# Attention, then two feed-forward layers on one core: the queries of two batches in one tile, and the epsilon and reciprocal of several head pairs in one instruction each

## The chip, the cores and the metric

The kernel runs on one NeuronCore of a Trainium2 chip. TensorE (PE in the views; PEld is its weight load), VectorE (DVE), ScalarE (ACT) and GpSimd (POOL) compute, SyncE (SP) issues the DMAs. The metric is device microseconds of one execution; before the change the median of three runs is 859.54 us (859.41 to 859.98).

## The reference, cut to what matters

```
q_s = exp(q - max(q, axis=-1)); q_s /= sum(q_s, axis=-1) + 1e-9     # over the 64 of a head
k_s = exp(k - max(k, axis=2));  k_s /= sum(k_s, axis=2) + 1e-9      # over the sequence
kv  = einsum('bhsd,bhse->bhde', k_s, v)                             # 64 x 64 per head
out = einsum('bhsd,bhde->bhse', q_s, kv)                            # 4 batches, 8 heads, 576 x 64
x   = out as 2304 tokens x 512
h = x @ w_in1;  x = (h * sigmoid(h)) @ w_out1                       # 512 -> 2048 -> 512
h = x @ w_in2;  y = (h * tanh(softplus(h))) @ w_out2
```

## The kernel before

**Tiling.** Eight heads are worked as four pairs (`hp` 0 to 3), so that 2 x 64 fills 128 partitions. The 2304 tokens are cut into six blocks of 384. A batch has 576 tokens, so block 1 holds 192 tokens of batch 0 and 192 of batch 1, block 4 those of batches 2 and 3; the other four lie within one batch. Weights and activations are split into a high and a low part, so that each product is three TensorE passes. In the first half of layer 1 a block needs eight groups of hidden units: for each group a first product "G1" (12 matmuls of 128x384, `psum<-xs,wall`), ScalarE's SiLU (`gf<-psum`), VectorE's high part (`CAST g`) and low part (`TENSOR_TENSOR g`), and a second product "G2" (12 matmuls, `psum<-g,wall`). I call them matmuls of the layer, and number the groups c0 to c7.

**Order.** `events` writes out G1 and G2 with G2 three groups behind G1 (`SKEW`), and each has a time in steps (`at`). Attention of the next blocks is a generator (`attn_steps`) whose pieces get times from `PACE`; a scheduler fixes the order on each engine from these times when the program is built, and then every engine works in order. The first block's attention is written out by hand in `START`. While block 0 is computed, the 16 weight pieces of the half are loaded (four buffers `st`, issued by SP in order), put together from two integer halves and split (`TENSOR_SCALAR st`, `ACTIVATE wt`, `SCALAR_TENSOR_TENSOR wt`, `CAST wall`, `TENSOR_TENSOR wall`): five instructions for each piece. Attention of block 1 runs in the same stretch, and block 1's G1 can't begin before it is done.

**Attention of a block.** `load` issues K, Q and V of a head pair. `front` (two head pairs at a time, four for block 2) turns K on TensorE, takes its maximum on VectorE (`knm`), the exponential with its sum on ScalarE (`kT_exp`, `kz`), and for the queries the maximum (`qmx`, VectorE), the subtraction (GpSimd) and the exponential (ScalarE). `back` takes a head pair: it turns the exponential of K back (`ke_turn`, `ke_copy`), forms `kv` on TensorE (`kv_prod`) and scales it (`kvf`, VectorE), sums the queries (`qz`, `qrz`, VectorE), divides (`qn`, GpSimd), turns (`qT`) and multiplies them with `kvf`. SiLU and the exponential are of different ScalarE tables, so going from one to the other puts an `ACT_TABLE_LOAD` into ScalarE's order.

Two buffers bind the order: G1 writes two PSUM banks in turn, `banks("h1", (4, 5))`, so G1 of group c waits for `gf` of group c-2; and `gf` has two buffers, so `gf` of c waits for the low part of c-2. Where a block has queries of two batches, each batch's queries are a tile of 96x256 of their own, and each is summed by

```
V.tensor_reduce(out=z, in_=qt, op=ALU.add, axis=AX.X)
V.tensor_scalar(out=z, in0=z, scalar1=EPS, scalar2=None, op0=ALU.add)
V.reciprocal(out=rz, in_=z)
```

Of the kernel before, what the change touches and what calls it, by code (L numbers as in the profile page):

```python
# [7 lines left out]
F32 = mybir.dt.float32  # L8
# [3 lines left out]
ALU = mybir.AluOpType  # L12
# [3 lines left out]
EPS = 1e-9  # L16
# [49 lines left out]
def attention_silu_mish(ctx: ExitStack, tc: tile.TileContext, q, k, v, w_in1, w_out1, w_in2, w_out2, out):  # L66
# [28 lines left out]
    TURN = 2  # L95


    X_LEAD, W_LEAD, T_LAG, P_LAG, A_END = 7, 8.0, 3.0, 4.0, 8.0
    X_NEAR = SKEW + 2


    W_EVERY, W_WAIT = 4.0, 8
    PACE = (0.5, 1.05)

    START = """
        A0 A1 M0 M1 Q0 B0 K0 B1 A2 C0 M2 A3 P2 M3 Q1 K1
        S0 E0 P4 R0 P3 C1 B2 Q2 K2 P2 Z0 B3 Q3 S1 N0 E1
        Z2 D1 S2 Z3 R1 C2 S3 Z1 N1 T0 E2 D0 K3 T1 R2 E3
        F0 U0 N2 X0 R3 C3 D2 U1 N3 F1 H0 T2 Y0 L0 T3 D3
        F2 F3 U2 U3 P2 X1 H1 Y1 X3 L1 H3 Y3 X2 H2 L3 L2  # L110
        Y2
    """.split()

    const = ctx.enter_context(tc.tile_pool(name="const", bufs=1))
# [243 lines left out]
    def room(parts, n):  # L358
        at = first["at"]
        first["at"] += n  # L360
        return xb[:parts, at:at + n]
# [34 lines left out]
            SP.dma_start(va[:, h, :, 0:D], v[b, 2 * hp + h].rearrange("(p r) d -> p r d", r=KR))  # L396
        return va

    def load_q(j, b, hp, s0, pn, rn):
        n = 2 * rn * D  # L400
        if j == 0:
            qt = room(pn, n)
        elif j == 1:
            qt = later(xb, hp, NT - (1 + (s0 == 0)) * n, pn, n)
        elif j == 2:
            qt = later(xa, hp, 3 * BLK, pn, n)
        else:
            qt = qp_.tile([pn, n], F32, tag="qt", name="qt")
        qt = qt.rearrange("p (h r d) -> p h r d", h=2, d=D)
        SP.dma_start(  # L410
            qt.rearrange("p h r d -> p h (r d)"),
            q[b, 2 * hp:2 * hp + 2, s0:s0 + pn * rn].rearrange("h (p r) d -> p h (r d)", r=rn),
        )
        return qt


# [11 lines left out]
        V.tensor_reduce(out=nm, in_=kT, op=ALU.max, axis=AX.XY, negate=True)  # L428
        return nm

    def kT_exp(kT, nm, hp):
        ek = spare_ek(hp)
        z = sp_.tile([P, 1], F32, tag="kz", name="kz")
        last = S.activation(
            out=ek.rearrange("p (i n) -> p i n", i=2), in_=kT, func=ACTF.Exp, bias=nm, accum_out=z
        )
        return ek, z, last

    def kT_sum(z):
        V.tensor_scalar(out=z, in0=z, scalar1=EPS, scalar2=None, op0=ALU.add)  # L440
        rz = sp_.tile([P, 1], F32, tag="krz", name="krz")
        V.reciprocal(out=rz, in_=z)
        return rz

# [56 lines left out]
        t = qt.rearrange("p h r d -> p (h r d)")  # L501
        S.activation(out=t, in_=t, func=ACTF.Exp)

    def q_sum(qt):
        z = sp_.tile(list(qt.shape[:3]), F32, tag="qz", name="qz")
        V.tensor_reduce(out=z, in_=qt, op=ALU.add, axis=AX.X)
        V.tensor_scalar(out=z, in0=z, scalar1=EPS, scalar2=None, op0=ALU.add)
        rz = sp_.tile(list(qt.shape[:3]), F32, tag="qrz", name="qrz")
        V.reciprocal(out=rz, in_=z)
        return rz  # L510

    def q_norm(qt, rz, qn=None):
        pn, _, rn, _ = qt.shape
# [37 lines left out]
    def attn_start():  # L551

        n = BLK
        rn = n // P
        kt, qt, va = {}, {}, {}
        for hp in range(NP):
            kt[hp] = load_k(0, hp)
        for hp in range(NP):
            qt[hp] = load_q(0, 0, hp, 0, P, rn)
# [3 lines left out]
        qn = [room(P, 2 * rn * D) for _ in range(NP)]  # L563
        st = {}

        def step(what, hp):
            def do(f, *args):
                st[what, hp] = f(*args)

            def got(what):  # L570
                return st[what, hp]

            if what == "A":
                do(kT_turn, kt[hp])
            elif what == "M":
                do(kT_max, got("A"))
            elif what == "B":
                do(kT_exp, got("A"), got("M"), hp)
            elif what == "Z":
                do(kT_sum, got("B")[1])  # L580
            elif what == "K":
                do(ke_turn, got("B")[0])
            elif what == "C":
                do(ke_copy, got("K"), kt[hp])
            elif what == "D":
                do(kv_prod, kt[hp], va[hp])
            elif what == "F":
                kvs[(0, hp)] = kv_scale(got("D"), got("Z"))
            elif what == "Q":
                do(q_max, qt[hp])  # L590
            elif what == "S":
                do(q_sub, qt[hp], got("Q"))
            elif what == "E":
                do(q_exp, qt[hp])
            elif what == "R":
                do(q_sum, qt[hp])
# [26 lines left out]
        InOrder.on = False  # L623
# [4 lines left out]
    def attn_steps(j, new, parts):  # L628

        turn = new is not None and new < TURN  # L630
        ld, mid = {}, {}

        def load(hp):
            kt = load_k(new, hp) if new is not None else None
            qs = [load_q(j, b, hp, s0, *shape(n)) for b, s0, n in parts]
            va = load_v(new, hp) if new is not None else None
            ld[hp] = (kt, va, qs)

        def front(hps):
            last = None  # L640
            for hp in hps:
                kt, va, qs = ld[hp]
                if turn:
                    kT = kT_turn(kt)
                    ek, z, last = kT_exp(kT, kT_max(kT), hp)
                    mid[hp] = ek, kT_sum(z)
                elif kt is not None:
                    k_max(kt)
                for qt in qs:
                    q_sub(qt, q_max(qt))  # L650
                yield
            for hp in hps:
                kt, va, qs = ld[hp]
                if kt is not None and not turn:
                    last = k_exp(kt)
            with tc.issue_after(last.ins) if last is not None else ExitStack():
                for hp in hps:
                    for qt in ld[hp][2]:
                        q_exp(qt)

        def back(hp):
            kt, va, qs = ld[hp]
            rz = None
# [4 lines left out]
            qn = q_norm(qs[0], q_sum(qs[0]))
            if kt is not None:
                kvs[(new, hp)] = kv_scale(kv_prod(kt, va), rz)  # L670
                yield
            for i, (b, s0, n) in enumerate(parts):
                cur = qn
                if i + 1 < len(parts):
                    qn = q_norm(qs[i + 1], q_sum(qs[i + 1]))
                base = tc.cur_priority
                tc.cur_priority = base + int(1000 * T_LAG)
                t = q_copy(q_turn(cur))
                tc.cur_priority = base + int(1000 * P_LAG)
                px = x_prod(t, kvs[(b, hp)])  # L680
                rn, t0 = cur.shape[1], b * SEQ + s0
                S.copy(tokens(xaT[:, hp, t0:t0 + n], rn), queries(px, rn))
                tc.cur_priority = base
                yield

        wide = NP if j == 2 else 2
        for hp in range(wide):
            load(hp)
        for h0 in range(0, NP, wide):
            yield from front(range(h0, h0 + wide))  # L690
            yield
            for hp in range(h0, h0 + wide):
# [407 lines left out]
```

## Time and profile before

| | |
|---|---|
| median of three runs | 859.54 us (859.41 to 859.98) |
| the profiled execution | 862.39 us, of which 859.1 us is the span from the first to the last instruction |
| TensorE busy | 842.5 us, 98% of the span, granted clock 1.00 |
| VectorE busy | 467.4 us, 54% |
| ScalarE busy | 364.6 us, 42% |
| GpSimd busy | 54.3 us, 6% |

A row of a timeline begins with the start (us from the span's start) and the duration; `x12` merges twelve like instructions; the bracket tells how long the engine was idle just before and which instruction ended that. The shapes of matmuls are those of the two operands; some merged rows count a transposition twice, as weight and as data.

### The profile page before, as it was taken

How to read it: one execution, taken by the hardware profiler on the slowest of the kernel's cores; microseconds unless marked ns; L12 is line 12 of the kernel's file. 1: busy time of each engine (PE TensorE's matmuls, PEld its weight loads, DVE VectorE, ACT ScalarE, POOL GpSimd, SP SyncE). 2: the span in 40 equal slices, each digit the busy share in tenths (PEclk: the TensorE clock that was granted, in tenths of full speed). 3: DMA queues.
4: the chain of work that ended last, by engine and by line, in shares of the span. 5: the costliest groups of instructions: out<-in, count | busy, mean ns of one | idle time of the engine just before them, and what ended most of it. 6: DMA issues, size and time to landing. Idle time of an engine off the chain costs nothing.

```text
span 859.1 us, 12311 instructions
## 1 busy us (share of the span) xinstructions
PE 842.5 (98%) x4666; PEld 755.1 (88%) x4666; DVE 467.4 (54%) x1004; ACT 364.6 (42%) x702; POOL 54.3 (6%) x82
## 2 busy tenths in 40 slices
PE   7899999999999999999999999999999999999998
PEld 6688989899999887898888899998999998999996
DVE  4998556673257556556474656675343454343431
ACT  5987354555244644435434444444322233322221
POOL 3144211221000000000000000000000000000000
PEclk9999999999999999999999999999999999999999
DMA  9995411120023428675632778889555455664312
GB/s 227 249 261 109 100 32 44 47 65 1 1 74 124 147 88 288 204 252 165 218 128 88 273 275 302 296 323 340 216 172 232 152 204 184 232 219 161 135 50 98
DMA packets 86105, 145.49 MB, mean 169 GB/s; under 512 B 33056, under 2 KB 60192, under 8 KB 82976
## 3 DMA queue, kind: packets, MB, share of 16 engines
q1 hardware_dynamic: 86048, 144.73, 51.9%
q8 instruction: 36, 0.59, 0.3%
q14 instruction: 21, 0.17, 0.1%
HBM read 105.38 MB, written 39.32 MB: 168 GB/s over the span
## 4 chain that ended last, share of the span: by engine, by line
PE 87%; DVE 5%; DMA 3%; ACT 2%; SPq 1%; issue 1%; ACTq 0%; DVEq 0%
PE psum L59 70%; PE psum L57 17%; DMA st<-in_moe_w_in_dram 2%; SPq L57 1%; DMA st<-in_moe_w_out_dram 1%; DVE g L57 1%; DVE qz L57 1%; DVE kmx L57 1%; DVE wall L57 0%; ACT xa L57 0%; DVE wt L59 0%; DVE st L57 0%; DVE xs L59 0%; DVE wt L57 0%; DVE xs L57 0%
## 5 line engine op out<-in xcount | busy, mean ns | idle before, releaser
L59 PE MATMUL psum<-wall,g 128*128 128x512 f32 x864 | 210.1, 390 | 0.0
L59 PE MATMUL psum<-x,wall 128*128 128x384 f32 x1008 | 191.8, 338 | 0.0
L59 PEld LDWEIGHTS psum<-wall,g 128*128 128x128 f32 x864 | 161.3, 188 | 28.5 <-DVE xb L59 0.3
L59 PEld LDWEIGHTS psum<-x,wall 128*128 128x128 f32 x1008 | 179.9, 187 | 6.8
L59 PE MATMUL psum<-g,wall 128*128 128x512 f32 (+2 forms) x624 | 129.0, 360 | 0.0
L59 PE MATMUL psum<-xs,wall 128*128 128x512 f32 (+2 forms) x588 | 122.7, 362 | 0.5 <-ACT gf L59 0.5
L59 PEld LDWEIGHTS psum<-g,wall 128*128 128x128 f32 x624 | 109.0, 188 | 14.7
L59 PEld LDWEIGHTS psum<-xs,wall 128*128 128x128 f32 x588 | 102.7, 188 | 15.8 <-ACT gf L59 0.9
L59 DVE TENSOR_TENSOR hf<-psum,sc 128x384 f32<-128x384 f32 x72 | 40.0, 556 | 123.4 <-ACT sc L59 79.0
L57 PE MATMUL psum<-xs,wall 128*128 128x384 f32 x468 | 98.3, 350 | 2.7 <-ACT gf L57 1.9
L59 ACT COPY sc<-psum 128x384 f32<-128x384 f32 x72 | 34.5, 479 | 133.0 <-PE psum L59 133.0
L57 PEld LDWEIGHTS psum<-xs,wall 128*128 128x128 f32 x468 | 80.3, 189 | 6.8 <-ACT gf L57 2.8
L57 PE MATMUL psum<-g,wall 128*128 128x384 f32 x432 | 84.8, 343 | 1.3 <-DVE g L57 1.3
L57 PEld LDWEIGHTS psum<-g,wall 128*128 128x128 f32 x432 | 74.7, 188 | 2.7 <-DVE g L57 1.8
L59 ACT ACTIVATE hf<-hf 128x384 f32<-128x384 f32 x72 | 37.8, 526 | 84.6 <-DVE hf L59 84.6
L59 DVE TENSOR_TENSOR g<-gf,g 128x512 fp32r<-128x512 f32 (+2 forms) x49 | 30.5, 623 | 74.7 <-ACT g L59 74.4
L59 ACT ACTIVATE gf<-psum 128x512 f32<-128x512 f32 (+2 forms) x49 | 26.6, 543 | 98.4 <-PE psum L59 97.4
L59 DVE CAST g<-hf 128x384 fp32r<-128x384 f32 x96 | 34.6, 360 | 58.1 <-ACT hf L59 57.7
L59 DVE TENSOR_TENSOR g<-hf,g 128x384 fp32r<-128x384 f32 x96 | 53.6, 559 | 3.3
L59 ACT ACTIVATE wt<-st 128x512 f32<-128x512 f32 x48 | 32.0, 676 | 19.5 <-DMA st<-in_moe_w_in_dram 10.7
L57 DVE CAST g<-gf 128x384 fp32r<-128x384 f32 x39 | 16.7, 427 | 38.7 <-ACT gf L57 38.6
L57 ACT ACTIVATE gf<-psum 128x384 f32<-128x384 f32 x39 | 18.9, 491 | 41.0 <-PE psum L57 39.3
(123 smaller groups left out, 747.1 us busy)
## 6 DMA issues: line engine op xcount, KB each, us to landing
wall<-wq SPq DMA_DIRECT2D x16, 1792.0 KB, 7.4
st<-in_moe_w_in_dram SPq DMA_DIRECT2D x32, 512.0 KB, 5.2
st<-in_moe_w_out_dram SPq DMA_DIRECT2D x32, 512.0 KB, 4.3
wall<-wo SPq DMA_DIRECT2D x32, 512.0 KB, 3.6
wq<-wall SPq DMA_DIRECT2D x8, 1792.0 KB, 6.2
wo<-wall SPq DMA_DIRECT2D x16, 512.0 KB, 5.6
wqf<-wt SPq DMA_DIRECT2D x24, 256.0 KB, 3.3
wall<-wqf SPq DMA_DIRECT2D x24, 256.0 KB, 6.5
```

The costliest lines, as they stand in the source:

```text
L57: return call(*args, **kwargs)
L59: self.last = call(*args, **kwargs)
```

## The change

1. `load_q` puts the queries of both batches of a block into one tile (96x512 in place of two of 96x256), still with one DMA each. Maximum, subtraction, exponential and sum of such a tile are then one instruction in place of two.
2. The epsilon and the reciprocal of the K sums are taken for two head pairs at once (`inverse`, 128x2), and those of the query sums for all head pairs that `front` takes together: 96x16 for blocks 1 and 4, 128x12 for 3 and 5, 128x24 for block 2. `q_sums` is called at the first of them, so no head pair's queries are divided before all of them have their exponential.
3. Constants of the order: `X_LEAD` 7 to 6, `PACE` (0.5, 1.05) to (0.35, 1.05), and the table `START` is written anew from its third line on.

```
-    X_LEAD, W_LEAD, T_LAG, P_LAG, A_END = 7, 8.0, 3.0, 4.0, 8.0
+    X_LEAD, W_LEAD, T_LAG, P_LAG, A_END = 6, 8.0, 3.0, 4.0, 8.0
-    PACE = (0.5, 1.05)
+    PACE = (0.35, 1.05)
...
-        Z2 D1 S2 Z3 R1 C2 S3 Z1 N1 T0 E2 D0 K3 T1 R2 E3
+        Z2 D1 S2 R1 C2 S3 N1 T0 E2 D0 F0 K3 T1 R2 E3 U0
...
-    def load_q(j, b, hp, s0, pn, rn):
+    def load_q(j, hp, parts, pn, rn):
         n = 2 * rn * D
+        m = len(parts) * n
...
+            qt = qp_.tile([pn, m], F32, tag="qt", name="qt")
+        qt = qt.rearrange("p (h r d) -> p h r d", r=rn, d=D)
+        for i, (b, s0, _) in enumerate(parts):
+            SP.dma_start(
+                qt[:, 2 * i:2 * i + 2].rearrange("p h r d -> p h (r d)"),
...
-    def kT_sum(z):
+    def inverse(z, tag):
         V.tensor_scalar(out=z, in0=z, scalar1=EPS, scalar2=None, op0=ALU.add)
-        rz = sp_.tile([P, 1], F32, tag="krz", name="krz")
+        rz = sp_.tile(list(z.shape), F32, tag=tag, name=tag)
         V.reciprocal(out=rz, in_=z)
...
-    def q_sum(qt):
-        z = sp_.tile(list(qt.shape[:3]), F32, tag="qz", name="qz")
-        V.tensor_reduce(out=z, in_=qt, op=ALU.add, axis=AX.X)
-        V.tensor_scalar(out=z, in0=z, scalar1=EPS, scalar2=None, op0=ALU.add)
...
+    def q_sums(qts):
+        h, r = qts[0].shape[1:3]
+        z = sp_.tile([qts[0].shape[0], len(qts), h * r], F32, tag="qz", name="qz")
+        for i, qt in enumerate(qts):
+            V.tensor_reduce(out=z[:, i].rearrange("p (h r) -> p h r", r=r), in_=qt, op=ALU.add, axis=AX.X)
+        rz = inverse(z, "qrz")
...
     def front(hps):
...
-                for qt in qs:
-                    q_sub(qt, q_max(qt))
+                q_sub(qt, q_max(qt))
                 yield
+            if turn:
+                rz = inverse(z, "krz")
+                for hp in hps:
+                    mid[hp] = mid[hp], rz[:, hp - hps[0]:hp - hps[0] + 1]
...
-        def back(hp):
+        def back(hp, hps):
...
-            qn = q_norm(qs[0], q_sum(qs[0]))
+            if hp == hps[0]:
+                qz.update(zip(hps, q_sums([ld[i][2] for i in hps])))
+            zq = qz.pop(hp)
+            qn = q_norm(qt[:, :2], zq[:, :2])
...
-                    qn = q_norm(qs[i + 1], q_sum(qs[i + 1]))
+                    qn = q_norm(qt[:, 2 * i + 2:2 * i + 4], zq[:, 2 * i + 2:2 * i + 4])
```

What this makes of the order, engine by engine: the orders differ from the first block's attention up to the 709th matmul of the layer (in block 3) and are the same behind it. Counted over the program, VectorE has 62 instructions fewer, GpSimd 8 and ScalarE 8 fewer, but ScalarE has 27 table loads in place of 23.

Place 1 is ScalarE in block 0. `xb,kz<-psum,knm` is the exponential of K of block 1's second head pair, `xb<-xb` that of its queries, `gf` the SiLU. Before, the first `gf` here is that of c2 and the last that of c3:

```order
L57 ACT_TABLE_LOAD
L57 ACTIVATE gf<-psum 128x384
L57 ACT_TABLE_LOAD
L57 ACTIVATE xb,kz<-psum,knm 128x576
L57 ACTIVATE xb<-xb 96x256 x3
L57 CAST wall<-wt 128x512
L57 ACTIVATE xb<-xb 96x256
L57 COPY xa<-psum 96x768
L57 ACTIVATE wt<-st 128x512 x3
L57 CAST wall<-wt 128x512
L57 ACT_TABLE_LOAD
L57 ACTIVATE gf<-psum 128x384
```

After the change the three `gf` are those of c1, c2 and c3:

```order
L57 ACT_TABLE_LOAD
L57 ACTIVATE gf<-psum 128x384
L57 ACT_TABLE_LOAD
L57 ACTIVATE xb,kz<-psum,knm 128x576
L57 ACTIVATE xb<-xb 96x512 x2
L57 CAST wall<-wt 128x512
L57 COPY xa<-psum 96x768
L57 ACTIVATE wt<-st 128x512 x2
L57 ACT_TABLE_LOAD
L57 ACTIVATE gf<-psum 128x384
L57 CAST wall<-wt 128x512 x2
L57 ACTIVATE gf<-psum 128x384
```

So the SiLU of c2 has moved from ahead of the second head pair's exponentials to behind them.

Place 2 is TensorE in the same stretch. `ident,xa` turns K, `ident,xb` turns its exponential back, `xb,xa` is `kv`. Eight matmuls of the layer stand ahead of these rows. Before:

```order
L57 MATMUL psum<-xs,wall 128x384 x19
L57 MATMUL psum<-ident,xa 128x96 x6
L57 MATMUL psum<-xs,wall 128x384 x21
L57 MATMUL psum<-g,wall 128x384 x8
L57 MATMUL psum<-ident,xa 128x96 x6
L57 MATMUL psum<-g,wall 128x384 x7
L57 MATMUL psum<-xs,wall 128x384 x12
L57 MATMUL psum<-g,wall 128x384
L57 MATMUL psum<-ident,xb 96x128 x6
L57 MATMUL psum<-g,wall 128x384 x10
L57 MATMUL psum<-xb,xa 64x64 x12
```

After the change (ahead of these rows stand 17 matmuls of the layer and the first head pair's turning of K):

```order
L57 MATMUL psum<-xs,wall 128x384 x19
L57 MATMUL psum<-g,wall 128x384 x7
L57 MATMUL psum<-ident,xa 128x96 x6
L57 MATMUL psum<-g,wall 128x384 x5
L57 MATMUL psum<-xs,wall 128x384 x12
L57 MATMUL psum<-g,wall 128x384
L57 MATMUL psum<-ident,xb 96x128 x6
L57 MATMUL psum<-g,wall 128x384 x9
L57 MATMUL psum<-xb,xa 64x64 x12
L57 MATMUL psum<-g,wall 128x384
L57 MATMUL psum<-ident,qn 128x96 x2
L57 MATMUL psum<-g,wall 128x384
```

The first G2 stood behind 48 matmuls of G1 and stands behind 36; the first `kv` of block 1 stood behind 86 matmuls of the layer and stands behind 70.

Place 3 is VectorE where the first two head pairs of block 1 are summed. Before:

```order
L57 TENSOR_SCALAR kz<-kz 128x1
L57 TENSOR_REDUCE qz<-xb 96x4
L57 RECIPROCAL krz<-kz 128x1
L57 TENSOR_REDUCE qz<-xb 96x4
L57 TENSOR_SCALAR qz<-qz 96x4
L57 TENSOR_REDUCE qz<-xb 96x4
L57 RECIPROCAL qrz<-qz 96x4
L57 TENSOR_TENSOR wall<-wt,wall 128x512
L57 TENSOR_SCALAR qz<-qz 96x4
L57 TENSOR_SCALAR st<-st 128x512
L57 RECIPROCAL qrz<-qz 96x4
L57 TENSOR_SCALAR qz<-qz 96x4
```

After the change (what stood further up or down for the same two head pairs before is in these rows now):

```order
L57 TENSOR_SCALAR kz<-kz 128x2
L57 TENSOR_SCALAR st<-st 128x512
L57 RECIPROCAL krz<-kz 128x2
L57 TENSOR_REDUCE qz<-xb 96x8 x2
L57 TENSOR_TENSOR wall<-wt,wall 128x512
L57 TENSOR_SCALAR qz<-qz 96x16
L57 TENSOR_SCALAR st<-st 128x512
L57 RECIPROCAL qrz<-qz 96x16
```

For these two head pairs four sums have become two, and six pairs of epsilon and reciprocal two.

## Rows read from the trace of the kernel before

**Rows 1.** The page: busy time of each engine, and forty slices of the span.

```profile
PE 842.5 (98%) x4666; PEld 755.1 (88%) x4666; DVE 467.4 (54%) x1004; ACT 364.6 (42%) x702; POOL 54.3 (6%) x82
...
PE   7899999999999999999999999999999999999998
```

**Rows 2.** Stages: us, busy PE, PEld, DVE, ACT, POOL, clock, DMA share, GB/s.

```profile
52.63:85.69 33.06, 31.28 (x242) 26.80 (x242) 29.57 (x73) 25.30 (x54) 15.41 (x20) 1.00 0.71 163
41.57:85.69 44.12, 41.63 (x324) 36.42 (x324) 40.56 (x103) 35.76 (x71) 19.33 (x25) 1.00 0.78 189
...
150.00:200.00 50.00, 49.70 (x362) 45.95 (x361) 33.52 (x94) 29.42 (x54) 12.42 (x19) 1.00 0.20 49
```

**Rows 3.** Timeline of TensorE, blocks 0 and 1.

```profile
39.38 0.86 PE L57 MATMUL psum<-g,wall 128*128 128x384 f32 x4
41.57 0.97 PE L57 MATMUL psum<-g,wall 128*128 128x384 f32 x4 [1.33 <-DVE g L57]
44.12 2.24 PE L57 MATMUL psum<-xs,wall 128*128 128x384 f32 x12
52.63 1.68 PE L57 MATMUL psum<-xs,wall 128*128 128x384 f32 x8 [0.72 <-ACT gf L57]
83.10 0.59 PE L57 MATMUL psum<-qT,kvf 128*128 128x192 f32 x2 [0.73 <-DVE kvf L57]
85.69 3.53 PE L57 MATMUL psum<-xs,wall 128*128 128x384 f32 x18
95.44 2.24 PE L57 MATMUL psum<-xs,wall 128*128 128x384 f32 x12
97.52 2.24 PE L57 MATMUL psum<-g,wall 128*128 128x384 f32 x12
```

**Rows 4.** Timeline of VectorE, block 0.

```profile
40.20 0.43 DVE L57 TENSOR_SCALAR st<-st 128x512 uint32<-128x512 uint32 x1 [0.36 <-DMA st<-in_moe_w_out_dram]
40.55 0.97 DVE L57 TENSOR_TENSOR g<-gf,g 128x384 fp32r<-128x384 f32 x1
43.07 0.76 DVE L57 TENSOR_REDUCE knm<-psum 128x1 f32<-128x576 f32 x1
46.38 0.42 DVE L57 TENSOR_REDUCE qz<-xb 96x4 f32<-96x256 f32 x1
46.71 0.15 DVE L57 RECIPROCAL krz<-kz 128x1 f32<-128x1 f32 x1
46.78 0.40 DVE L57 TENSOR_REDUCE qz<-xb 96x4 f32<-96x256 f32 x1
48.16 0.57 DVE L57 TENSOR_SCALAR qz<-qz 96x4 f32<-96x4 f32 x1
```

**Rows 5.** Timeline of ScalarE, block 0, and one row of block 3.

```profile
42.88 0.49 ACT L57 ACTIVATE gf<-psum 128x384 f32<-128x384 f32 x1
43.91 1.28 ACT L57 ACT_TABLE_LOAD   x1 [0.53 <-DVE knm L57]
45.20 0.74 ACT L57 ACTIVATE xb<-psum,knm 128x576 f32<-128x576 f32 x1
45.93 1.02 ACT L57 ACTIVATE xb<-xb 96x256 f32<-96x256 f32 x3
46.85 0.61 ACT L57 CAST wall<-wt 128x512 fp32r<-128x512 f32 x1
47.68 0.79 ACT L57 COPY xa<-psum 96x768 f32<-96x768 f32 x1
48.37 1.83 ACT L57 ACTIVATE wt<-st 128x512 f32<-128x512 f32 x3
50.80 1.28 ACT L57 ACT_TABLE_LOAD   x1
52.09 0.49 ACT L57 ACTIVATE gf<-psum 128x384 f32<-128x384 f32 x1
...
173.24 0.49 ACT L57 ACTIVATE gf<-psum 128x384 f32<-128x384 f32 x1 [0.70 <-PE psum L57]
```

More of the change, by code (lines that the diff above doesn't have):

```diff
@@ L107, in attention_silu_mish @@
         S0 E0 P4 R0 P3 C1 B2 Q2 K2 P2 Z0 B3 Q3 S1 N0 E1
-        Z2 D1 S2 Z3 R1 C2 S3 Z1 N1 T0 E2 D0 K3 T1 R2 E3
-        F0 U0 N2 X0 R3 C3 D2 U1 N3 F1 H0 T2 Y0 L0 T3 D3
-        F2 F3 U2 U3 P2 X1 H1 Y1 X3 L1 H3 Y3 X2 H2 L3 L2
-        Y2
+        Z2 D1 S2 R1 C2 S3 N1 T0 E2 D0 F0 K3 T1 R2 E3 U0
+        N2 X0 R3 C3 D2 U1 N3 F1 H0 T2 Y0 L0 T3 D3 F2 F3
+        U2 U3 P2 X1 H1 L1 Y1 X3 H3 Y3 X2 H2 L3 L2 Y2
     """.split()
@@ L397, in load_v @@
         return va
-    def load_q(j, b, hp, s0, pn, rn):
+    def load_q(j, hp, parts, pn, rn):
         n = 2 * rn * D
+        m = len(parts) * n
         if j == 0:
-            qt = room(pn, n)
+            qt = room(pn, m)
         elif j == 1:
-            qt = later(xb, hp, NT - (1 + (s0 == 0)) * n, pn, n)
+            qt = later(xb, hp, NT - m, pn, m)
         elif j == 2:
-            qt = later(xa, hp, 3 * BLK, pn, n)
+            qt = later(xa, hp, 3 * BLK, pn, m)
         else:
[L408 to L413, printed above, removed]
+            qt = qp_.tile([pn, m], F32, tag="qt", name="qt")
[3 more added lines that the diff above has]
+                qt[:, 2 * i:2 * i + 2].rearrange("p h r d -> p h (r d)"),
+                q[b, 2 * hp:2 * hp + 2, s0:s0 + pn * rn].rearrange("h (p r) d -> p h (r d)", r=rn),
+            )
         return qt
@@ L429, in kT_max, with kT_exp @@
         return nm
-    def kT_exp(kT, nm, hp):
+    def kT_exp(kT, nm, hp, z):
         ek = spare_ek(hp)
-        z = sp_.tile([P, 1], F32, tag="kz", name="kz")
         last = S.activation(
@@ L436, in kT_exp @@
         )
-        return ek, z, last
-    def kT_sum(z):
+        return ek, last
+    def inverse(z, tag):
         V.tensor_scalar(out=z, in0=z, scalar1=EPS, scalar2=None, op0=ALU.add)
-        rz = sp_.tile([P, 1], F32, tag="krz", name="krz")
+        rz = sp_.tile(list(z.shape), F32, tag=tag, name=tag)
         V.reciprocal(out=rz, in_=z)
@@ L502, in q_exp @@
         S.activation(out=t, in_=t, func=ACTF.Exp)
-    def q_sum(qt):
-        z = sp_.tile(list(qt.shape[:3]), F32, tag="qz", name="qz")
-        V.tensor_reduce(out=z, in_=qt, op=ALU.add, axis=AX.X)
-        V.tensor_scalar(out=z, in0=z, scalar1=EPS, scalar2=None, op0=ALU.add)
-        rz = sp_.tile(list(qt.shape[:3]), F32, tag="qrz", name="qrz")
-        V.reciprocal(out=rz, in_=z)
-        return rz
+    def q_sums(qts):
[4 more added lines that the diff above has]
+        rz = inverse(z, "qrz")
+        return [rz[:, i].rearrange("p (h r) -> p h r", r=r) for i in range(len(qts))]
     def q_norm(qt, rz, qn=None):
@@ L558, in attn_start @@
         for hp in range(NP):
-            qt[hp] = load_q(0, 0, hp, 0, P, rn)
+            qt[hp] = load_q(0, hp, [(0, 0, n)], P, rn)
         for hp in range(NP):
@@ L563, in attn_start @@
         qn = [room(P, 2 * rn * D) for _ in range(NP)]
+        kz = sp_.tile([P, NP], F32, tag="kz", name="kz")
         st = {}
@@ L577, in step @@
             elif what == "B":
-                do(kT_exp, got("A"), got("M"), hp)
+                do(kT_exp, got("A"), got("M"), hp, kz[:, hp:hp + 1])
             elif what == "Z":
-                do(kT_sum, got("B")[1])
+                rz = inverse(kz[:, hp:hp + 2], f"krz{hp}")
+                st["Z", hp], st["Z", hp + 1] = rz[:, :1], rz[:, 1:]
             elif what == "K":
@@ L595, in step @@
             elif what == "R":
-                do(q_sum, qt[hp])
+                st["R", hp], = q_sums([qt[hp]])
             elif what == "N":
@@ L630, in attn_steps @@
         turn = new is not None and new < TURN
-        ld, mid = {}, {}
+        ld, mid, qz = {}, {}, {}
         def load(hp):
             kt = load_k(new, hp) if new is not None else None
-            qs = [load_q(j, b, hp, s0, *shape(n)) for b, s0, n in parts]
+            qt = load_q(j, hp, parts, *shape(parts[0][2]))
             va = load_v(new, hp) if new is not None else None
-            ld[hp] = (kt, va, qs)
+            ld[hp] = (kt, va, qt)
         def front(hps):
@@ L641, in front @@
             for hp in hps:
-                kt, va, qs = ld[hp]
+                kt, va, qt = ld[hp]
                 if turn:
                     kT = kT_turn(kt)
-                    ek, z, last = kT_exp(kT, kT_max(kT), hp)
-                    mid[hp] = ek, kT_sum(z)
+                    if hp == hps[0]:
+                        z = sp_.tile([P, len(hps)], F32, tag="kz", name="kz")
+                    ek, last = kT_exp(kT, kT_max(kT), hp, z[:, hp - hps[0]:hp - hps[0] + 1])
+                    mid[hp] = ek
                 elif kt is not None:
                     k_max(kt)
-                for qt in qs:
-                    q_sub(qt, q_max(qt))
+                q_sub(qt, q_max(qt))
                 yield
+            if turn:
+                rz = inverse(z, "krz")
+                for hp in hps:
+                    mid[hp] = mid[hp], rz[:, hp - hps[0]:hp - hps[0] + 1]
             for hp in hps:
-                kt, va, qs = ld[hp]
+                kt, va, qt = ld[hp]
                 if kt is not None and not turn:
@@ L657, in front @@
                 for hp in hps:
-                    for qt in ld[hp][2]:
-                        q_exp(qt)
-        def back(hp):
-            kt, va, qs = ld[hp]
+                    q_exp(ld[hp][2])
+        def back(hp, hps):
+            kt, va, qt = ld[hp]
             rz = None
@@ L667, in back @@
                 yield
[L668 removed]
+            if hp == hps[0]:
+                qz.update(zip(hps, q_sums([ld[i][2] for i in hps])))
+            zq = qz.pop(hp)
+            qn = q_norm(qt[:, :2], zq[:, :2])
             if kt is not None:
@@ L692, in attn_steps @@
             for hp in range(h0, h0 + wide):
-                yield from back(hp)
+                yield from back(hp, range(h0, h0 + wide))
                 if hp + wide < NP:
```

## The prediction

> **What bounds the kernel now.** I read the page first. TensorE is busy for 98% of the span, and its first slice apart its busy digits are 8 and 9 all the way [rows 1]. 859.1 - 842.5 leaves 16.6 us of idle time, and only in it can this change find anything, because it takes no matmul away. So the next view is busy time by stage [rows 2]: between 150 and 200 us, where blocks 2 and 3 run with attention beside them, TensorE idles for 0.3 us of 50. From 41.57 to 85.69 it idles for 44.12 - 41.63 = 2.5 us while VectorE is busy for 40.56 of 44.12 and ScalarE for 35.76. That is block 0, with 16 weight pieces to put together and block 1's attention to finish. The change has to pay there or nowhere.
>
> The timeline of TensorE shows what the idle time waits for [rows 3]: 1.33 us ahead of 41.57 for the first group's low part, which stands on VectorE behind a weight piece that landed at 40.20 [rows 4]; 0.72 us ahead of 52.63 for a SiLU; 0.73 us ahead of 83.10 for a `kvf`. From 85.69 on the matmuls of the layer follow at full pace, twelve in 97.52 - 95.44 = 2.08 us, 0.1733 us each.
>
> I take 85.69 as the marker. By the order, 198 matmuls of the layer and all of block 1's attention are then done, and some of block 2's: five transpositions and one product, which take about 1.2 us up to 85.69. Without those the stretch would have ended at 84.5. From there TensorE is the bound in both kernels and does the same work, so what the marker shifts, the end shifts.
>
> **What the change removes.** In block 1's attention VectorE loses 16 of the small instructions (4 for K, 12 for the queries). One takes 0.07 to 0.09 us from start to start (46.71 to 46.78) [rows 4]; by 0.08 that is 1.3 us. Eight pairs of 96x256 reductions become eight of 96x512. One takes 46.71 - 46.38 = 0.33 us; 96x512 is not in the trace, so it lies between 0.33 and 0.66, and I take 0.60, since the length in elements is most of the price at this size: 8 x 0.06 = 0.5 us. Block 2's attention loses six more small ones, 0.5 us. Sum 2.3 us of VectorE up to the marker. The four saved in `START` are worth nothing: VectorE waits for the first weight piece right behind them. Blocks 3 to 5 lose as much again, where VectorE is busy for 33.52 of 50 us [rows 2]: nothing, as the matmuls cover it.
>
> At 48.16 one small instruction takes 0.57 us, where one at 46.71 takes 0.15 [rows 4], while GpSimd works. Half as many GpSimd instructions, each up to twice as long, can make that better or worse by up to half a us; I count 0.
>
> Where rule and row must be weighed: the Trainium skill, Perfetto Trace Analysis, "Optimizing Scalar/DVE Operations", says that larger operations help a saturated engine, and that breaking operations up can help where VectorE or ScalarE isn't saturated but makes others wait. The first half would put the gain at the whole 2.3 us; the second speaks against merging, and no row here decides between them.
>
> **What the new order adds.** This is the term that eats the gain. Up to the first group's low part nothing gets much earlier: it still stands behind the ninth weight piece. On TensorE 48 + 4 matmuls of the layer stood ahead of that wait, and now 36 + 4 do. Behind it, the SiLU of c2 was the next thing of ScalarE at 42.88 [rows 5], and G1 of c4 began at 44.12 [rows 3]. Now that SiLU stands behind the second head pair's exponentials. Its chain, by rows:
> - 41.57 to 43.07, rest of G2 and the turning of K up to `knm`: 1.5 us; one matmul fewer now, so 1.3 [rows 3, 4]
> - `knm` 0.76 [rows 4], table load 1.28, exponential of K 0.74 [rows 5]
> - two exponentials of 96x512: three of 96x256 take 0.92 us from start to start, so 0.31 each; twice that is the upper bound and 0.31 the lower; I take 0.55 each, 1.1
> - cast 0.51, copy 0.69, two weight activations at 0.6 each 1.2, table load 1.28, SiLU 0.49 [rows 5]
>
> Sum 9.35 us. From the low part at 41.5 that is 50.8. The ninth piece's DMA is issued when the fifth piece has been put together, which now has one piece's work less ahead of it, so the low part may come up to 0.7 us earlier: G1 of c4 begins between 50.1 and 50.8, and I take 50.5.
>
> By the order 72 matmuls of the layer are done at that moment. Before, 96 were at 52.63. So 126 are left to the marker, and not 102. The rest is taken from the stage 52.63 to 85.69 [rows 2]: busy 31.28, less 102 x 0.1733 = 17.7, less block 2's 1.2, is 12.4 us of attention, which does not change. The marker then lies at 50.5 + 126 x 0.1733 + 12.4 = 84.7 plus whatever TensorE waits behind 50.5. Before, it waited 33.06 - 31.28 = 1.8 us in that stage. It should wait less: VectorE has 2.3 us less to do in a stage in which it had 3.5 us to spare, and the last `kvf` now stands behind 179 matmuls of the layer in place of 197. But some of the waits are ScalarE's. Between 0 and 1.8 I take 0.6. Marker 85.3, against 84.5: 0.8 us later. The attention is ahead, the matmuls of the layer are behind, and the saving on VectorE fills the difference nearly.
>
> **Block 3.** Four more table loads, 4 x 1.28 = 5.1 us of ScalarE, all in the stage in which it is busy for 29.42 of 50 us. The SiLU of c0 in block 3, at 173.24 before [rows 5], now has an exponential of block 5's queries and two loads ahead of it. Its bank is needed by G1 of c2, some 2.5 us behind it (an estimate: the twelve matmuls of c1 at 0.1733 and two or three of attention). I count 0 and give the case a chance below. The Trainium skill, ScalarE: Activation LUTs, "What ACT_TABLE_LOAD costs", gives about 2.66 us for each switch, a drain included; the row of 43.91 shows the exponential begin 1.29 us later, so the rows bear out 1.28, and by the page the four would come to 10.6 us.
>
> **Sum.** The profiled execution was 862.39 us, span 859.1, so 3.3 us lie around the span, and it stands 2.85 us above the median. Its span would become 859.1 + 0.8 = 859.9. Set on the median of 859.54 that is 860.3 us. What a measurement of this kernel can tell from no change is about 0.2%, 1.7 us; I forecast no change that can be told.
>
> **The rivals.**
> - VectorE decides: it is busy for 92% of the stretch, and if its order, not TensorE's, sets when block 1 may begin, the 2.3 us come off whole, and TensorE makes up the matmuls in waits that go. For it: the 1.33 and 0.73 us are both waits for VectorE. Against it: TensorE needs 84.7 us by the sum above without any wait. It needs G1 of c4 by 49 us. 859.54 - 2.3 = 857.2 us. Chance 0.24.
> - The late SiLU decides: G1 of c4 begins at 51.4 or later (a ninth piece that lands late, since the K loads now stand ahead of two weight pieces in SP's order), and TensorE waits as long behind it as before, 1.8 us. Marker 51.4 + 21.8 + 12.4 + 1.8 = 87.4, 2.9 us late: 862.4 us. It decides from G1 of c4 at 51.4 with 0.8 us of waits. For it: the ScalarE chain has no slack. Chance 0.22.
> - The table loads of block 3 decide: if block 5's queries arrive 2 us after ScalarE's turn comes, the SiLUs of c0 and c1, G1 of c2 and c3 wait in turn. A load, an exponential and a load, 1.28 + 0.55 + 1.28 = 3.1 us, less 2.5 of slack, and the 2 us of lateness: about 2.6 us on top of 0.8, 862.9 us. Against it: these loads depend on tiles that come free early. Chance 0.07.
>
> **How the numbers follow.** The forecast, 860.3 us, has 0.47; its own range is 858.6 to 861.3. The range reaches to both sides, from 856.8 (2.3 us and half a us fewer collisions on VectorE off 859.54) to 863.0, just past the last rival. Faster by over 0.2% (under 857.8) is the first rival, 0.24; slower by over 0.2% (above 861.3) the other two, 0.29; the rest is within 0.2%, 0.47.
>
> **What would show it.** In the profile after: G1 of c4 (the first matmuls `psum<-xs,wall` behind the first `qn` transpositions) at about 50.5, with an idle time ahead of it that waits for a SiLU; an idle time of some 3 us on TensorE ahead of the first G2, near 38 to 41 us; VectorE's busy time about 4 us lower over the span; the first G1 of block 1 about 82 to 83 us, with 48 matmuls in one run; no idle time over 0.3 us in block 3. I am wrong if G1 of c4 begins before 49.5 or the span is below 857.3, and on the other side if TensorE waits for more than 1.5 us between 50 and 86 us.

## The result: slower, and the profile after

The changed kernel takes 866.71 us (median of six executions, 863.53 to 867.50), the kernel before beside it 859.59 us; the ratio is 1.0067, 95% interval 1.0056 to 1.0078. That is slower, above the range given. (The two medians alone lie further apart, by 7.1 us or 0.83%; the table below uses the ratio.) The profiled execution took 864.52 us with a span of 862.7, 3.6 us more than before. All six executions have a mean granted clock of 0.994 to 0.996; the profiled one before had 0.999.

The page of the changed kernel, busy time of each engine and the first slices of the span (compare [rows 1]):

```profile
PE 844.1 (98%) x4666; PEld 758.0 (88%) x4666; DVE 464.6 (54%) x942; ACT 369.7 (43%) x698; POOL 50.1 (6%) x74
...
PE   8799999999999999999999999999999999999998
```

VectorE is busy for 2.8 us less and TensorE for 1.6 us more, though it has the same matmuls. So some of them ran slower. Busy time by stage, with the granted clock in the third column from the right, tells which (the first three rows are from a table by single us):

```profile
38.00:39.00 1.00, 0.00 (x0) 0.00 (x0) 0.92 (x2) 0.95 (x3) 0.00 (x0) 1.00 1.29 195
40.00:41.00 1.00, 0.30 (x1) 0.30 (x2) 0.97 (x3) 0.98 (x2) 0.10 (x1) 0.50 1.17 208
46.00:47.00 1.00, 1.00 (x6) 1.00 (x6) 1.00 (x1) 0.99 (x2) 0.83 (x1) 0.84 1.24 197
...
40.70:46.30 5.60, 5.60 (x20) 5.50 (x21) 3.70 (x7) 2.58 (x3) 0.51 (x1) 0.50 1.15 250
52.92:88.39 35.47, 32.84 (x253) 29.30 (x254) 29.94 (x55) 25.64 (x53) 8.88 (x14) 1.00 0.71 177
150.00:200.00 50.00, 49.79 (x377) 45.94 (x378) 29.05 (x70) 31.93 (x52) 10.67 (x16) 1.00 0.20 46
```

From about 39.5 to 46.3 us the granted clock is 0.50, the lower of TensorE's two levels, 1.2 GHz in place of 2.4. Block 3, where the four added table loads lie, is undisturbed: 0.21 us idle in 50. TensorE's timeline of the changed kernel, against [rows 3]:

```profile
34.49 2.37 PE L57 MATMUL psum<-xs,wall 128*128 128x384 f32 x12 [1.11 <-ACT gf L57]
40.70 2.61 PE L57 MATMUL psum<-g,wall 128*128 128x384 f32 x7 [3.85 <-DVE g L57]
43.11 1.16 PE L57 MATMUL psum<-ident,xa 96*128 96x96 f32 x6
43.98 1.95 PE L57 MATMUL psum<-g,wall 128*128 128x384 f32 x5
52.92 2.01 PE L57 MATMUL psum<-xs,wall 128*128 128x384 f32 x10 [0.66 <-ACT gf L57]
85.21 0.59 PE L57 MATMUL psum<-qT,kvf 128*128 128x192 f32 x2 [1.87 <-DVE kvf L57]
88.39 8.48 PE L57 MATMUL psum<-xs,wall 128*128 128x384 f32 x48
```

The 3.85 us ahead of the first G2 are the idle time that was expected there. Behind it seven G2 matmuls take 43.11 - 40.70 = 2.41 us, 0.344 each; at the full clock one takes 0.1733 [rows 3]. The turning of the second head pair's K is late by that, VectorE's `knm` with it, and with `knm` ScalarE's chain up to the SiLU of c2. G1 of c4 begins at 52.92. A second large wait, 1.87 us, stands at the end of block 0 ahead of the last products of block 1's attention. VectorE ahead of the first G2 before the change (one row), and then at both places in the changed kernel:

```profile
35.05 0.35 DVE L57 CAST g<-gf 128x384 fp32r<-128x384 f32 x1
...
39.61 0.77 DVE L57 TENSOR_SCALAR st<-st 128x512 uint32<-128x512 uint32 x1 [0.69 <-DMA st<-in_moe_w_out_dram]
40.30 0.35 DVE L57 CAST g<-gf 128x384 fp32r<-128x384 f32 x1
44.31 0.76 DVE L57 TENSOR_REDUCE knm<-psum 128x1 f32<-128x576 f32 x1 [1.86 <-PE psum L57]
...
80.63 1.52 DVE L57 TENSOR_REDUCE kmx<-xa 96x128 f32<-96x768 f32 x1
83.45 1.44 DVE L57 TENSOR_REDUCE kmx<-xa 96x128 f32<-96x768 f32 x1
84.81 0.34 DVE L57 SCALAR_TENSOR_TENSOR kvf<-psum,krz,mask 128x128 f32<-128x128 f32 x1
```

The first group's high part (`CAST g`) now stands behind an instruction that waits for the ninth weight piece. Before, it was done 5 us ahead of that instruction (40.20 [rows 4]), and the low part alone waited. The last `kvf` stands behind the two maxima of block 3's K, 1.44 us each.

### The profile page after: what moved, and what is told of

It is laid out like the page before. It is cut to its first block, busy times and chain, and to the rows that moved or that the text cites. A ratio compares the mean times of both kernels' runs of the same rounds, so it can differ in the third digit from the quotient of the medians.

```text
span 862.7 us, 12217 instructions
## 1 busy us (share of the span) xinstructions
PE 844.1 (98%) x4666; PEld 758.0 (88%) x4666; DVE 464.6 (54%) x942; ACT 369.7 (43%) x698; POOL 50.1 (6%) x74
## 4 chain that ended last, share of the span: by engine, by line
PE 92%; DVE 3%; DMA 2%; ACT 1%; SPq 1%; issue 1%; POOL 0%; ACTq 0%; DVEq 0%; POOLq 0%
PE psum L59 72%; PE psum L57 20%; SPq L57 1%; DMA st<-in_moe_w_in_dram 1%; DMA st<-in_moe_w_out_dram 1%; DVE kmx L57 1%; DVE g L57 0%; ACT xa L57 0%; DMA xb<-in_k_dram 0%; ACT wt L57 0%; DVE wall L57 0%; DVE xs L57 0%; DVE st L57 0%; ACT wall L57 0%; DVE qz L59 0%
## 5 line engine op out<-in xcount | busy, mean ns | idle before, releaser
L57 PE MATMUL psum<-g,wall 128*128 128x384 f32 x432 | 88.5, 350 | 3.8 <-DVE g L57 3.8
```

The costliest lines, as they stand in the source:

```text
L57: return call(*args, **kwargs)
```

## The experiments

Sixteen kernels were each timed against the kernel before on the same chip. Since the mean granted clock differs between executions of one kernel, the table gives its span over them, and the median span (from first to last instruction) of those executions whose clock was 0.999 or 1.000, "at the full clock". The kernel before has 857.8 us there on the first chip (53 of 75 executions) and 857.5 on the second (16 of 29), on which the last four ran.

| run | ratio to before, 95% interval | clock | span at the full clock |
|---|---|---|---|
| the change | 1.0067 (1.0056 to 1.0078) | 0.994 to 0.996 | none |
| e1 16 spare products | 1.0056 (1.0040 to 1.0071) | 0.994 to 0.998 | none |
| e2 24 spare products | 1.0069 (1.0044 to 1.0094) | 0.994 to 0.999 | 860.9 (2 of 6) |
| e3 old START | 1.0026 (1.0012 to 1.0040) | 0.994 to 1.000 | 859.7 (8 of 11) |
| e4 order alone | 1.0052 (1.0037 to 1.0067) | 0.995 to 1.000 | 861.6 (1 of 6) |
| e5 ninth piece | 1.0057 (1.0038 to 1.0076) | 0.991 to 0.999 | 860.3 (1 of 9) |
| e6 eighth and ninth | 1.0049 (1.0032 to 1.0066) | 0.994 to 1.000 | 860.9 (2 of 9) |
| e7 kmx late | 1.0029 (1.0014 to 1.0044) | 0.993 to 1.000 | 858.7 (1 of 12) |
| e8 merges alone | 1.0027 (1.0016 to 1.0039) | 0.998 to 1.000 | 861.0 (10 of 12) |
| e9 tiles alone | 1.0005 (0.9996 to 1.0014) | 0.997 to 1.000 | 858.3 (7 of 11) |
| e10 block 2 apart | 1.0007 (0.9998 to 1.0016) | 0.998 to 1.000 | 858.7 (8 of 11) |
| e11 before, ninth piece | 0.9999 (0.9990 to 1.0007) | 0.999 to 1.000 | 857.9 (11 of 11) |
| e12 before, ninth and kmx | 0.9990 (0.9981 to 0.9999) | 0.999 to 1.000 | 857.0 (11 of 11) |
| e13 START alone | 1.0070 (1.0046 to 1.0094) | 0.994 to 0.998 | none |
| e14 PACE alone | 0.9992 (0.9981 to 1.0003) | 0.997 to 1.000 | 857.4 (8 of 12) |
| e15 change, both moves | 1.0029 (1.0016 to 1.0043) | 0.993 to 1.000 | 858.5 (3 of 12) |
| e16 merges, both moves | 1.0008 (0.9998 to 1.0018) | 0.998 to 1.000 | 859.4 (11 of 12) |

**Which part of the change.** In the changed kernel the table `START` goes back to that of before, less its two merged steps (e3), or all three constants do (e8). In the kernel before all three are new (e4), START alone (e13), or PACE alone (e14).

```
e3   START: Z2 D1 S2 R1 C2 S3 N1 T0 E2 D0 K3 ...      (the rest as before)
e8   e3, X_LEAD 7, PACE (0.5, 1.05)
e4   kernel before: X_LEAD 6, PACE (0.35, 1.05), START: Z2 D1 S2 Z3 R1 C2 S3 Z1 N1 T0 E2 D0 F0 K3 ...
e13  kernel before: START as in e4        e14  kernel before: PACE as in e4
```

> The changed kernel with the table START of before (less the two steps that are merged): both merges and the new pacing stay, and the first G2 stands behind 48 matmuls of G1 again. Theory A: an idle time of 1.3 to 2 us there, clock 1.00, 858 to 860.5 us. Rival C (the merges themselves delay block 1, since a head pair's queries wait for both sums): 862 us or more with the clock at 1.00. Rival B, too, expects this one at 860.

> The changed kernel with all three order constants of before (the two steps of START that are merged left out): the merges alone. Theory C (the merges cost something by themselves, since no head pair is divided before all that are taken together have their sums; block 2's sums of all four head pairs above all): waits of TensorE for GpSimd's qn of more than 1 us together near 75 and 91 us, 1 to 2 us above the kernel before at a clock of 1.00. Rival (merges are free or gain, the order alone costs): within 0.7 us of the kernel before, or up to 2 us below.

> The kernel before with the change's three order constants alone (the two steps of START that are separate there put back), and none of the merges. Theory A: first G2 behind 36 matmuls of G1, idle 3.5 us or more, granted clock 0.5 for 6 us or more, 864 to 868 us. Rival C: within 1 us of the kernel before.

> The kernel before with the new table START alone (its two separate steps put back). If START is what moves the first G2 ahead of the fourth G1 group: first G2 behind 36 matmuls of G1, idle 3.5 us or more ahead of it, a granted clock of 0.5 behind that in most executions, 863 to 866 us, as the run with all three constants. Rival (the pacing matters as much): 862 us or less.

> The kernel before with PACE 0.35 alone. If START is the cause: within 0.7 us of the kernel before, clock 0.998 to 1.00. Rival (the pacing brings block 1's attention into the same stretch too early): 1 us or more above it.

START alone costs as much as the whole change, 1.0070; PACE alone costs nothing. `X_LEAD` was not changed alone; START and PACE together with it (e4) cost no more than START. START puts the first G2 behind 36 matmuls of G1, and TensorE's row there in e13 reads

```profile
42.60 2.61 PE L57 MATMUL psum<-g,wall 128*128 128x384 f32 x7 [4.69 <-DVE kz L57]
```

with a granted clock of 0.50 around it, as in e4, where the idle time was 5.65 us. With the old START (e3, e8) the loss shrinks to 1.0026 and 1.0027, and for the larger part the clock stays up. At the full clock e8's span is 3.2 us longer than before, more than the 1 to 2 us expected. So there are two losses, START's and a smaller one of the merges, and they don't add. START's is not made up alike in every kernel: e13 waits longer ahead of the first G2 and not at all for the last `kvf`.

**Which merge.** e9 takes the epsilon and reciprocal of every head pair apart again and keeps the wide tiles; e10 takes only block 2's apart. Both have the order constants of before.

```
e9   back():  zq, = q_sums([qt])            front(): mid[hp] = ek, inverse(z, "krz")
e10  back():  if j == 2: qz[hp], = q_sums([qt])
              elif hp == hps[0]: ...
```

> Order constants of before, the queries of two batches in one tile, but epsilon and reciprocal for each head pair alone again. Theory C (the merged epsilon and reciprocal hold the first head pairs back): the waits for qn at 50.9, and at 90.6 in block 2, go; 1.5 to 3 us below the run with both merges, within 0.7 us of the kernel before. Rival E (the wide tile costs it: the maximum, the subtraction and the exponential of 96x512 come later than the first of two of 96x256): 1 us or less below the run with both merges, 2 us or more above the kernel before.

> Order constants of before and both merges, but block 2's epsilon and reciprocal for each of its four head pairs alone. Theory C in its narrow form (block 2's 128x24, which waits for the last head pair's queries, is the cost): no wait for qn over 0.3 us behind block 1's first 18 matmuls, about 1.5 us below the run with both merges, 861 to 861.8 us. Rival: that wait gives way to another, no change.

Without block 2's merged epsilon and reciprocal the loss can no longer be told from none (1.0007), and undoing the others adds nothing that can be told (1.0005). The place in e8, VectorE and then TensorE:

```profile
84.67 0.55 DVE L57 TENSOR_REDUCE qmx<-xa 128x6 f32<-128x384 f32 x1 [2.13 <-DMA xa<-in_q_dram]
87.54 0.54 DVE L57 TENSOR_REDUCE qz<-xa 128x6 f32<-128x384 f32 x1
88.45 0.43 DVE L57 TENSOR_SCALAR qz<-qz 128x24 f32<-128x24 f32 x1
88.92 0.30 DVE L57 RECIPROCAL qrz<-qz 128x24 f32<-128x24 f32 x1
...
90.59 0.55 PE L57 MATMUL psum<-ident,qn 128*128 128x128 f32 x3 [1.12 <-POOL qn L57]
```

The fourth head pair's queries land at 84.67; all four head pairs wait for them, and TensorE waits 1.12 us in the middle of block 1's matmuls. The median spans at the full clock differ by 2.3 us between e8 and e10, so this wait is about half of the loss; where the rest arises was not traced. In the changed kernel this transposition stands at 105.03, behind 96 matmuls of block 1, and waits for nothing.

**The idle time ahead of the first G2.** e1 and e2 put spare products into the changed kernel; e5 and e6 move the first instruction of the ninth, or of the eighth and ninth, weight piece behind the first group's low part (`issue_after` fixes the order on VectorE and adds no wait).

```
e1, e2  ahead of G2 of c0, 16 or 24 times (they change no result):
        T.matmul(psum[:, 3 * 512:3 * 512 + P], ident, ident, start=True, stop=True)
e5, e6  with tc.issue_after(g_low[0]) if 9 <= state["dec"] <= 9 else ExitStack():     # e6: 8 <= ... <= 8
            V.tensor_scalar(out=lo, in0=lo, scalar1=29, ...)
```

In e6 the ninth piece's instruction follows the eighth's by the order.

> The changed kernel with 16 spare products of the unit matrix, written to an unused part of PSUM, nine of them in the wait ahead of the third G1 group and four right ahead of the first G2; the order of everything else is unchanged. Theory A (the idle time of 3.85 us ahead of the first G2 lets TensorE's clock fall, and the half clock costs the time): granted clock 1.00 between 38 and 48 us, idle ahead of the first G2 about 2 us, G1 of c4 at 50.5 to 51.5, 860 to 862 us. Rival B (the SiLU of c2 behind the second head pair's exponentials costs it, the clock only happens beside it): clock up, G1 of c4 still near 52.5, 864 us or more.

> As the one with 16 spare products, with 24, of which twelve stand right ahead of the first G2, so that hardly any idle time is left there; the second head pair's K is turned six matmuls earlier. Theory A: the same time as with 16 or up to 1 us less, clock 1.00, 859.5 to 861.5 us. Rival B: 864 us or more. If the spare products delay the first G2, 0.5 us comes on top in either.

> The changed kernel with one instruction of VectorE moved: the first one of the ninth weight piece, which waits for that piece's DMA and holds up the first group's high and low part behind it, now stands behind these two. Nothing else changes but the place of two G2 matmuls. Theory A (the idle time ahead of the first G2 and the clock that falls in it): the first G2 at about 39.3 instead of 40.7, idle 2.4 us instead of 3.85, the clock falls in fewer executions, 861 to 864 us. Rival B (the chain of ScalarE up to the SiLU of c2, the clock aside): no better than 1.4 us below the changed kernel in the executions whose clock stays up, and 865 us over all.

> As the run with the ninth piece, with the first instruction of the eighth piece moved behind the first group's low part as well, so that VectorE waits for no DMA ahead of it. Theory A: the first G2 follows the third group of G1 at 36.9 to 38.5, idle below 1.5 us, granted clock 1.00 through block 0, G1 of c4 at 49.5 to 51, 859.5 to 862 us. Rival B: G1 of c4 stays beyond 51.5, 863 us or more. A third way (the pieces that wait longer now come late to G1 of c5): an idle time ahead of c5 as long as what was won, 864 us or more.

The spare products settled nothing. In e1's profiled execution the ninth piece landed at 40.95 in place of 39.61, so 3.03 us of idle time were left ahead of 41.70; the mean clocks are 0.994 to 0.998 all the same. In e2's profiled one the first G2 waits for nothing and the clock is 1.00 there, but it had fallen at 25 us, behind a wait of 1.99 us in the first block's attention. e5 missed too: its first G2 came at 39.89 behind 3.23 us of idle time, and the clock fell. e6 missed over all (865.07 us, where 859.5 to 862 were expected, and seven of nine executions below the full clock), but its profiled execution has the clock at 1.00 throughout:

```profile
39.29 2.36 PE L57 MATMUL psum<-g,wall 128*128 128x384 f32 x12 [2.45 <-DVE g L57]
50.77 2.02 PE L57 MATMUL psum<-xs,wall 128*128 128x384 f32 x10 [0.65 <-ACT gf L57]
83.16 0.59 PE L57 MATMUL psum<-qT,kvf 128*128 128x192 f32 x2 [1.89 <-DVE kvf L57]
86.34 8.48 PE L57 MATMUL psum<-xs,wall 128*128 128x384 f32 x48
```

G1 of c4 begins at 50.77, and the span is still 861.2: the clock is not the whole of it, and the wait for the last `kvf` stays. The 50.77 are not the clock's doing alone, since the first G2 began 1.41 us earlier than in the changed kernel.

**The end of block 0.** e7 moves the maxima of block 3's K behind block 1's last `kvf` in the changed kernel, e15 does so on top of e6. e11 is e5's move in the kernel before, e12 has both moves there, e16 both moves with the merges except block 2's and the order of before.

```
e7   with tc.issue_after(kv_ins[7]) if len(kv_ins) == 8 else ExitStack():
         V.tensor_reduce(out=km, in_=kt.rearrange("p r h d -> p (h d) r"), op=ALU.max, axis=AX.X)
```

> The changed kernel with the two maxima of block 3's K (1.44 us each on VectorE) behind block 1's last kvf instead of ahead of it; no other engine's order changes. Theory D (VectorE's order at the end of block 0 is what costs the second part): the 1.87 us ahead of the last products of block 1 become 0.3 or less, first G1 of block 1 at about 86.8 instead of 88.4, time 1 to 1.6 us below the changed kernel at the same clock, 864.5 to 865.5 over all. Rival: the kvf waits for its product or another engine, the idle time stays over 1.2 us, no difference.

> The changed kernel with both moves: the eighth and ninth weight piece's first instruction behind the first low part, and the maxima of block 3's K behind block 1's last kvf. If the two waits and the clock are the loss: 859 to 860 us of span at a full clock, 861 to 863 us over all, 3 to 5 us below the changed kernel. Rival (the late SiLU of c2 alone decides): 864 us or more.

> The kernel before with the first instruction of the ninth weight piece moved behind the first group's low part on VectorE, nothing else. If the idle time of 1.33 us ahead of 41.57 sets the end: 0.6 to 1.3 us below the kernel before. Rival (ScalarE's chain or a later weight piece takes its place): within 0.4 us.

> As the run of the kernel before with the ninth piece moved, with the maxima of block 3's K behind block 1's last kvf as well. If the 0.73 us ahead of 83.10 is VectorE's queue: another 0.5 to 1 us below that run. Rival: block 3's K comes too late, an idle time of 1 us or more between 100 and 150 us, no gain or a loss of up to 1 us.

> The order constants of before, both merges except in block 2, the ninth piece behind the first low part and the maxima of block 3's K behind the last kvf. If the merges save VectorE time that counts once those waits are gone: 857.5 to 859 us, below the kernel before with the two moves alone. Rival (they save time that nothing waits for): the same as that run, 859 us.

In e7 the wait is gone. First the timeline, VectorE and then TensorE's first G1 of block 1; below it busy time in the stage from G1 of c4 up to there:

```profile
82.00 0.34 DVE L57 SCALAR_TENSOR_TENSOR kvf<-psum,krz,mask 128x128 f32<-128x128 f32 x1
82.26 2.95 DVE L57 TENSOR_REDUCE kmx<-xa 96x128 f32<-96x768 f32 x2
...
85.78 8.48 PE L57 MATMUL psum<-xs,wall 128*128 128x384 f32 x48
```

```profile
52.42:85.78 33.36, 32.61 (x253) 29.22 (x254) 29.68 (x54) 25.62 (x53) 9.08 (x14) 1.00 0.77 180
```

TensorE idles for 0.75 us of this stage in place of 35.47 - 32.84 = 2.63. The ratio falls from 1.0067 to 1.0029, more than was expected of it, but the clock was higher as well (0.9965 in the mean of its executions, 0.9950 in the changed kernel's), so not all of that is the wait. e15 is no better than e7: 863.16 us, just above the 861 to 863 expected, and 858.5 of span at the full clock. In the kernel before, the ninth piece alone changes nothing: in e11 the wait ahead of the low part shrinks to 0.47, and the wait for a SiLU behind it, 0.72 us at 52.63 [rows 3], grows to 1.32. With the maxima late as well, e12 ends 0.1% below the kernel before, and its interval stays just below 1: the only version that beat both kernels, by very little. e16 was expected at 859 us or less and took 861.32, a ratio of 1.0008 against e12's 0.9990: the merges, even without block 2's, don't add to the gain but seem to take it back. Its profiled execution waits 0.62 us for a `qn` of block 1 at 49.20, which e12's does not; the rest was not traced.

## Why the prediction was wrong

**What bounds the kernel** held: the whole difference arises up to the first G1 of block 1, and blocks 2 and 3 run alike (TensorE idles for 0.21 us here, 0.3 before [rows 2]).

**The idle time ahead of the first G2** was foreseen at some 3 us, near 38 to 41; it is 3.85 us, ahead of 40.70. That nothing would follow from it but its length is the first step that failed. The sum took "rest of G2 and the turning of K up to `knm`" as 1.3 us; from 40.70 to 44.31 it took 3.6, all of it at a granted clock of 0.50. Not all of that is the clock's. The prediction let four G2 matmuls (its "36 + 4") go ahead of the wait; they came behind it, because the high part waited too. At the full clock the seven G2 matmuls and the turning would take about 7 x 0.1733 + 0.70 = 1.9 us, so the clock cost 1.7 us here. This is an estimate; the 0.70 is the time before from the turning (42.37, the first row below, TensorE before the change) to `knm` (43.07 [rows 4]). The chain would have reached `knm` at 42.6, where 50.5 less the 8.05 us that follow `knm` in the sum gives 42.5. The rest of ScalarE's chain, from `knm` to G1 of c4, took 52.92 - 44.31 = 8.61 us where the terms give 9.35 - 1.3 = 8.05. Each of its prices, the 1.28 of a table load and 0.55 of an exponential of 96x512, was about right (two take 1.14 in a row); half of the excess is a wait for TensorE that the terms don't have (the second row, ScalarE in the changed kernel):

```profile
42.37 0.66 PE L57 MATMUL psum<-ident,xa 96*128 96x96 f32 x6
...
49.11 0.80 ACT L57 COPY xa<-psum 96x768 f32<-96x768 f32 x1 [0.29 <-PE psum L57]
```

So G1 of c4 came at 52.92 and not at 50.5: 1.7 us of the 2.4 by the clock, 0.6 by the rest of the chain. The Trainium skill, TensorE: Matmul & The Clock Gate, "The HAM clock gate (the "warmup" mystery)", says that TensorE's clock falls to 1.2 GHz when the engine stands idle and comes back once it is busy again; the trace agrees, with 0.50 from 39.5 to 46.3 us behind idle time that began at 36.86. That rule belonged among the rivals and was not there.

**The term for waits** is the second step that failed. From G1 of c4 to the first G1 of block 1 the sum has 120 x 0.1733 + 12.4 = 33.2 us of work, and 32.84 were measured; but TensorE waits 2.63 us in this stage, not the 0.6 taken "between 0 and 1.8", because VectorE had "2.3 us less to do". VectorE's total was no measure of it: 1.87 us of the wait is one `kvf` in VectorE's queue behind two maxima of block 3, and e7, which changes that queue alone, has 0.75 us. So the first G1 of block 1 should have come at 50.5 + 33.2 + 0.6 = 84.3 (the "82 to 83" among the signs does not follow from the sum) and came at 88.39: 2.4 us by the late G1 of c4, 2.0 by the waits, 0.4 less by the work. The span grew by 3.6, where 0.8 was forecast; the sign of being wrong, waits of over 1.5 us between 50 and 86, came true. Without these two losses the sum was near: at the full clock and with the maxima late, e7 and e15 are 0.9 and 1.0 us of span above the kernel before (one and three executions), where the sum has 0.8.

**The rivals.** The second, "the late SiLU decides", has the place and the sign (G1 of c4 beyond 51.4, waits as before, 862.4 us). But without the clock's 1.7 us G1 of c4 would have come at about 51.2, just short of the 51.4 that the rival asks for: the SiLU was late for another reason in the main, and the rival's price was passed. The first rival is refuted: the merges by themselves gained nothing, and cost 1.0027. That goes back to the 2.3 us of VectorE that the sum takes off: the saving is real (2.8 us less busy time over the span, where about 4 were forecast), but nothing waits for it. Its condition, G1 of c4 by 49 us, is also 1 us off: a marker at 84.5 - 2.3 = 82.2 leaves 82.2 - 21.8 - 12.4 = 48.0. And merging made one instruction wait for four head pairs: the sum counted instructions and not what each one must wait for. The third, table loads in block 3, didn't come.

**The rule that was weighed.** The Trainium skill, Perfetto Trace Analysis, "Optimizing Scalar/DVE Operations", says that breaking operations up can help where an unsaturated VectorE makes others wait. The runs agree for block 2: VectorE is idle for 2.13 us ahead of 84.67 in e8, and taking the merge apart brings 1.0027 to 1.0007 in e10.

**What the clock costs over all executions.** The medians of the span at the full clock give the order's share, at 860.9 in e6 against 857.8: about 3 us. The other share can be read in e6 too: its seven executions below the full clock have a median span of 863.5, 2.6 us above the two at it. Over the executions of all the kernels, compared within each kernel, 0.001 less of mean clock goes with about 0.65 us more of span, and the change's mean of 0.9950 against 0.9991 before gives 2.7 us by that. Together with the order's share it is some 5.7 us, near the 5.8 us of the ratio and short of the 7.1 us between the medians. This sum is an estimate; it takes e6's order for the change's, whose clocks are lower. That START's order brings the lower clock is shown by e13 against the kernel before; that it does so by the idle time ahead of the first G2 is argued. For it: in all seven profiled executions with 3.03 to 5.65 us of idle time there (the change, e1, e4, e5, e7, e13, e15) the clock fell in that wait or at most 1.1 us behind it, and in e6's, with 2.45, it did not. Against it: e1, e2 and e5, which were to show it, didn't hold the clock up over their executions, and the clock also fell behind shorter waits (1.2 to 2.0 us) in the profiled executions of e2, e3 and e14. What decides it stays open.

## What to carry to other kernels

Before an order is changed, find each wait that it lengthens on TensorE, and count with its length and, as a rival, a stretch at half the clock behind it. A saving of busy time on an engine is worth what the instruction that others wait for moves, so look at what stands ahead of that one instruction in its queue. Merging small instructions gained nothing here, and where the inputs arrive one after the other (block 2) all of them waited for the latest.

## What the runs showed of the hardware

Executions of one and the same program differ by the clock that was granted: e5's nine have 0.991 to 0.999, and spans of 867.1 to 860.3 us. e12's eleven keep within 2.0 us (856.3 to 858.3 us, 0.999 to 1.000), but the kernel before, whose profile shows no long gap either, has 0.996 to 1.000 and 856.6 to 861.5 us. So one profile doesn't tell what such a gap costs: the change's profiled execution took 864.52 us, its median is 866.71. In the profiled execution of e3 the clock fell within the second of two short waits of 1.16 and 1.24 us at 32 to 35 us, while the kernel before has one of 1.33 us ahead of 41.57 [rows 3] and kept 1.00 there. In the profiled execution of e14 it fell at about 35.3, behind a wait of 1.35 us ahead of 33.40, and its span was 859.5 where the median at the full clock is 857.4. The timeline of e3's TensorE, and below it its busy time and granted clock at the second wait and behind it:

```profile
33.07 0.79 PE L57 MATMUL psum<-xs,wall 128*128 128x384 f32 x3 [1.16 <-ACT gf L57]
35.10 1.22 PE L57 MATMUL psum<-ident,xa 96*128 96x96 f32 x6 [1.24 <-DMA xa<-in_k_dram]
```

```profile
34.00:35.00 1.00, 0.00 (x0) 0.00 (x0) 1.00 (x3) 0.04 (x1) 0.00 (x0) 0.70 1.05 221
35.00:36.00 1.00, 0.90 (x6) 0.90 (x7) 1.00 (x3) 0.73 (x2) 0.00 (x0) 0.50 1.03 261
36.00:41.00 5.00, 5.00 (x19) 5.00 (x18) 4.98 (x9) 4.22 (x7) 1.23 (x1) 0.50 1.20 206
```
